# One in-place ring of five long slots for a grouped 1x1 convolution that streams 201 MB

## Chip, cores, metric

The kernel runs on one core of a Trainium2 chip. The metric is the device time of one execution in microseconds (us); the executions of one kernel quoted here differ by 0.03 to 0.7% (0.1% before, 0.3% after the change). "Span" is the length of the one execution that the profiler recorded; it is 1.7 to 2.2 us shorter than the time of the same execution.

## The reference

```python
# x: (1, 512, 512, 192) bf16, w: (1, 1, 4, 48, 48) bf16, out as x
xg = x.reshape(1, 512, 512, 4, 48)
out = einsum('bhwgc,gcd->bhwgd', xg, w[0, 0])     # four groups of 48 channels, per pixel
```

It is a per-pixel product with a block-diagonal 192x192 matrix. There are 262,144 pixels of 384 bytes: 100.66 MB have to come in and 100.66 MB have to go out.

## The kernel before

Pixels lie in SBUF 128 rows deep. A "column" is one pixel of each of the 128 rows (49 KB), and there are 2,048 columns. TensorE transposes eight columns at a time (a "pair" of two groups of four columns), VectorE copies the transposed data out of PSUM, TensorE multiplies, and ScalarE (ACT) casts the result into an output buffer. SyncE (SP) issues the loads, ACT the stores. Input and output each have a ring of 256 columns, in pieces of 64 columns, with small pieces at both ends.

```python
BIG = 64                       # columns of a piece: 64*384 B = 24,576 B per row, one packet
RCOLS = 256                    # columns of each of the two rings
HEAD = (4, 4, 8, 16, 32)
TAIL = (32, 16, 8, 4, 4)
# ... plan_pieces: HEAD, then 30 pieces of BIG, then TAIL, for loads and for stores
def rows_view(ap, p):          # a piece's pixels: row r gets p.size neighbouring pixels
    return ap[128*p.col:128*(p.col+p.size), :].rearrange("(p i) c -> p (i c)", p=128)
# ...
x_sb = sbuf("x_sb", [128, RCOLS*C]);  o_sb = sbuf("o_sb", [128, RCOLS*C])
# SP: a load waits until TensorE has transposed what lay in its place
for p in loads:
    wq.wait(t_done, (p.g1 - body + 1) // 2)
    sp.dma_start(ring_view(x_sb, p), rows_view(xf, p)).then_inc(ld_sem[p.key], 16)
# ACT: a cast waits until the store of what lay in its place has landed
for g in range(NG):
    wait_out_free(wq, g)
    wq.wait(mm_done, g + 1)
    while pending and pending[0][1] <= g:
        store(pending.pop(0)[0])
    act.copy(dst_in_o_sb, o_ps[...]).then_inc(fa_done, 1)
    if g in store_end:
        pending.append((store_end[g], g + ST_DELAY))
```

Of the kernel before, what the change touches and what calls it, by code (L numbers as in the profile page):

```python
# [6 lines left out]
BF16 = mybir.dt.bfloat16  # L7
# [4 lines left out]
C = GROUPS * CG  # L12
UC = 2 * C
# [8 lines left out]
ESHIFT = 112  # L22
ECOLS = 272

BIG = 64
RCOLS = 256
HEAD = (4, 4, 8, 16, 32)
TAIL = (32, 16, 8, 4, 4)
NXP = 4
NXS = 3  # L30
NOB = 4
ST_DELAY = 2


class Waiter:

    def __init__(self, eng):
        self.eng = eng
        self.seen = {}
# [7 lines left out]

class Piece:

    def __init__(self, col, size, key):  # L50
        self.col, self.size, self.key = col, size, key
        self.g0, self.g1 = col // 4, (col + size) // 4


def plan_pieces(cols, head, tail):
    sizes = list(head) if cols >= sum(head) + sum(tail) else []
    last = list(tail) if sizes else []
    mid = cols - sum(sizes) - sum(last)
    pieces, c = [], 0
    for s in sizes + [BIG] * (mid // BIG) + ([mid % BIG] if mid % BIG else []) + last:  # L60
        whole = s == BIG and c % BIG == 0
        pieces.append(Piece(c, s, ("big", c // BIG % (RCOLS // BIG)) if whole else ("own", len(pieces))))
        c += s
    return pieces


def bass_standalone__grouped__vision_kernel(nc, x, w, out):
    B, H, W_, Cx = x.shape
    assert Cx == C and tuple(w.shape) == (1, 1, GROUPS, CG, CG)
    npix = B * H * W_  # L70

    cols = npix // 128
    assert npix % 512 == 0, "the pixel count must be a multiple of 512"
    NG = cols // 4
    loads = plan_pieces(cols, HEAD, TAIL)
    stores = plan_pieces(cols, HEAD, TAIL)
    load_of = {p.g0: p for p in loads}
    store_at = {g: p for p in stores for g in range(p.g0, p.g1)}
    store_end = {p.g1 - 1: p for p in stores}

    xf = x.rearrange("b h w c -> (b h w) c")
    of = out.rearrange("b h w c -> (b h w) c")
    wv = w.rearrange("a b g c d -> c (a b g) d")

    body = RCOLS // 4
    NP = (NG + 1) // 2

    def groups(pair):
        return range(2 * pair, min(2 * pair + 2, NG))

    def rows_view(ap, p):
        return ap[128 * p.col:128 * (p.col + p.size), :].rearrange("(p i) c -> p (i c)", p=128)

    def ring_view(t, p):
        at = p.col % RCOLS
        assert at + p.size <= RCOLS
        return t[:, at * C:(at + p.size) * C]

    with ExitStack() as es:
        block = es.enter_context(nc.Block())  # L100
        x_sb = es.enter_context(nc.sbuf_tensor("x_sb", [128, RCOLS * C], BF16))
        o_sb = es.enter_context(nc.sbuf_tensor("o_sb", [128, RCOLS * C], BF16))
        xT_sb = [es.enter_context(nc.sbuf_tensor(f"xT_sb{i}", [128, 4 * UC], BF16)) for i in range(NXS)]
        ident = es.enter_context(nc.sbuf_tensor("ident", [128, 128], BF16))
        esel = es.enter_context(nc.sbuf_tensor("esel", [CG, ECOLS], BF16))
# [5 lines left out]
        def sem(name):  # L111
            return es.enter_context(nc.semaphore(name))

        ld_sem = {k: sem(f"ld_{k[0]}{k[1]}") for k in dict.fromkeys(p.key for p in loads)}
        st_sem = {k: sem(f"st_{k[0]}{k[1]}") for k in dict.fromkeys(p.key for p in stores)}
        ld_val, st_val, seen = {}, {}, {}
        for p in loads:
            seen[p.key] = seen.get(p.key, 0) + 16
            ld_val[p] = seen[p.key]
        seen = {}  # L120
        for p in stores:
            seen[p.key] = seen.get(p.key, 0) + 16
            st_val[p] = seen[p.key]
        w_sem, id_sem, e_sem, wb_sem, wc_sem = (sem(s) for s in ("w_sem", "id_sem", "e_sem", "wb_sem", "wc_sem"))
        p0_sem, p1_sem = sem("p0_sem"), sem("p1_sem")
        t_done, mm_done = sem("t_done"), sem("mm_done")
        e_done, fa_done = sem("e_done"), sem("fa_done")

        def wait_out_free(wq, g):
            if g >= body:  # L130
                p = store_at[g - body]
                wq.wait(st_sem[p.key], st_val[p])

        @block.gpsimd
        def _(gp):
# [11 lines left out]
        @block.sync  # L147
        def _(sp):
            wq = Waiter(sp)
            sp.dma_start(w_sb[:], wv).then_inc(w_sem, 16)  # L150
            for p in loads:
                wq.wait(t_done, (p.g1 - body + 1) // 2)
                sp.dma_start(ring_view(x_sb, p), rows_view(xf, p)).then_inc(ld_sem[p.key], 16)  # L153

        @block.tensor
        def _(pe):
            wq = Waiter(pe)

            def build_weights():
                wq.wait(e_sem, 1)  # L160
                wq.wait(w_sem, 16)
                last = None
                for (tc, r, g, c0_) in WBLOCKS:
                    s0 = ESHIFT - r
                    col = WOFF[tc] + c0_
                    last = pe.matmul(o_ps[:, NOB - 1, col:col + CG], lhsT=esel[:, s0:s0 + 128],  # L166
                                     rhs=w_sb[:, g, :], start=True, stop=True, skip_group_check=True)
                last.then_inc(wb_sem, 1)

            def transposes(pair):  # L170
                wq.wait(e_done, pair - 1)
                last = None
                for g in groups(pair):
                    p = load_of.get(g)
                    if p:
                        wq.wait(ld_sem[p.key], ld_val[p])
                    for ul in range(2):
                        u = g % body * 2 + ul
                        for tc in range(3):
                            col = u * UC + tc * 128  # L180
                            j = ul * 3 + tc
                            last = pe.transpose(xT_ps[:, g % NXP, j * 128:(j + 1) * 128],  # L182
                                                x_sb[:, col:col + 128], ident[:])
                last.then_inc(t_done, 1)

            def matmuls(pair):
                wq.wait(e_done, pair + 1)
                for g in groups(pair):
                    xs = xT_sb[pair % NXS][:, g % 2 * 2 * UC:(g % 2 + 1) * 2 * UC]
                    wq.wait(fa_done, g - 1)  # L190
                    last = None
                    for ul in range(2):
                        v = 2 * g + ul
                        for tc in range(3):
                            j = ul * 3 + tc
                            c0_, c1_ = COLR[tc]
                            last = pe.matmul(o_ps[:, v % NOB, c0_:c1_], lhsT=xs[:, j * 128:(j + 1) * 128],  # L197
                                             rhs=wt[:, WOFF[tc]:WOFF[tc] + (c1_ - c0_)],
                                             start=(tc == 0), stop=(tc == 2), skip_group_check=True)
                    last.then_inc(mm_done, 1)  # L200

            build_weights()
            wq.wait(id_sem, 1)
            transposes(0)
            wq.wait(wc_sem, 1)
            for pair in range(NP):
                if pair + 1 < NP:
                    transposes(pair + 1)
                matmuls(pair)

        @block.vector
        def _(dve):
            wq = Waiter(dve)
            wq.wait(wb_sem, 1)
            dve.tensor_copy(wt[:], o_ps[:, NOB - 1, 0:WCOLS]).then_inc(wc_sem, 1)  # L215
            for pair in range(NP):
                n = len(groups(pair))
# [6 lines left out]
        @block.scalar  # L224
        def _(act):
            wq = Waiter(act)
            pending = []

            def store(p):
                act.dma_start(rows_view(of, p), ring_view(o_sb, p)).then_inc(st_sem[p.key], 16)  # L230

            for g in range(NG):
                wait_out_free(wq, g)
                wq.wait(mm_done, g + 1)
                while pending and pending[0][1] <= g:
                    store(pending.pop(0)[0])
                v = 2 * g
                u = g % body * 2
                dst = o_sb[:, u * UC:(u + 2) * UC].rearrange("p (u c) -> p u c", u=2)
                act.copy(dst, o_ps[:, v % NOB:v % NOB + 2, 0:UC]).then_inc(fa_done, 1)  # L240
                if g in store_end:
                    pending.append((store_end[g], g + ST_DELAY))
            for (p, _) in pending:
                wq.wait(fa_done, p.g1)
                store(p)
            for p in stores:
                if st_val[p] == seen[p.key]:
                    wq.wait(st_sem[p.key], st_val[p])


# [26 lines left out]
```

## Time and profile before

| | before |
|---|---|
| time, median (range) | 489.41 us (489.05 to 489.53, 4 runs) |
| span of the profiled run | 488.1 us |
| TensorE / ACT / VectorE busy | 90% / 79% / 50% |
| bytes moved / mean rate | 202.2 MB / 414 GB/s |

First the parts of the page of the kernel before that say what the transfers did: the span cut into 40 slices (DMA busy in tenths, then GB/s), the queues, and the head of the chain of waits that ended last. Queue 1 carries the loads, queue 10 the stores, queue 8 instructions.

```profile
span 488.1 us, 13741 instructions
DMA  8999999999999999999999999999999999999793
GB/s 291 421 428 433 432 424 430 430 428 434 430 429 420 436 421 438 424 436 426 430 428 429 432 426 430 432 424 434 424 434 427 426 434 428 419 430 401 334 388 147
...
q10 hardware_dynamic: 5760, 100.67, 48.5%
q1 hardware_dynamic: 5968, 100.68, 48.5%
q8 instruction: 49, 0.80, 0.6%
q14 instruction: 10, 0.07, 0.0%
...
DMA 76%; PE 17%; ACT 3%; another core or an unknown queue 1%; issue 1%; SPq 1%; ACTq 0%
```

The rate is flat near 429 GB/s from the second slice on and falls only in the last four. 201.3 MB at 429 GB/s take 469 us, so 19 of the 488 us are start and tail. The chain of waits is 76% transfers.

Now the tail, in the view by stretches of 10 us of the kernel before. The columns are: length, busy us of TensorE matmuls (PE), weight loads, VectorE, ACT and GpSimd with counts, the granted clock, the mean busy share of the 16 DMA engines, GB/s.

```profile
210.00:220.00 10.00, 8.10 (x100) 7.48 (x99) 3.83 (x4) 7.16 (x10) 0.00 (x0) 0.83 1.00 429
220.00:230.00 10.00, 9.46 (x140) 8.41 (x138) 5.75 (x6) 8.56 (x12) 0.00 (x0) 1.00 1.00 427
...
450.00:460.00 10.00, 9.80 (x148) 8.92 (x146) 5.80 (x7) 9.09 (x13) 0.00 (x0) 1.00 0.92 386
460.00:470.00 10.00, 9.80 (x148) 8.92 (x147) 5.80 (x7) 9.13 (x13) 0.00 (x0) 1.00 0.76 318
470.00:480.00 10.00, 5.76 (x60) 4.70 (x57) 2.39 (x3) 4.55 (x6) 0.00 (x0) 0.75 0.62 260
480.00:490.00 10.00, 0.98 (x6) 0.64 (x6) 0.00 (x0) 1.61 (x3) 0.00 (x0) 0.50 0.39 153
```

In the bulk TensorE's busy time and even its clock may drop (210 to 220 us) and the DMA share stays at 1.00: the transfers do not wait for the compute. In the tail the mean share sinks, so some of the 16 DMA engines are already idle while others still work.

Who waited for whom in the kernel before (us in total, times, longest), and how long transfers took from issue to landing (median us in the last column):

```profile
ACT o_sb L240 <- DMA out_dram<-o_sb: 35.5, 21, 2.3
PE xT_ps L182 <- DMA x_sb<-in_x_dram: 6.5, 3, 3.9
SPq L153 <- PE xT_ps L182: 400.2, 31, 16.3
...
x_sb<-in_x_dram SPq DMA_DIRECT2D x30, 3072.0 KB, 27.1
out_dram<-o_sb ACTq DMA_DIRECT2D x30, 3072.0 KB, 45.2
```

A 3 MB store needs about 7.3 us at 429 GB/s, but lands after 45 us: several are queued. With a queue that deep the DMA engines were not short of work: their share is 1.00 to 1.03 in every 10 us from 50 to 430 us.

The trace keeps 16 completions of every transfer, and among the packets 16 of 4 bytes for each (656 of queue 1 for 41 loads, 640 of queue 10 for 40 stores). The last completion of all comes at 487.6 us, 0.4 us after the last packet. The completions of the third-last full-size store before the change are, relative to their median: first -6.2 us, second-last +2.2 us, last +9.6 us. One engine is alone at the end, from 484.2 to 487.2 us.

### The profile page before, as it was taken

The page shows a single profiled execution, that of the slowest core. Times are in us where ns is not written, and L with a number is a line of the kernel's source. Part 1 is how long each engine was busy: PE and PEld are TensorE (multiplying, and loading weights), DVE is VectorE, ACT ScalarE, POOL GpSimd, SP SyncE. Part 2 cuts the span into 40 slices and gives each one's busy share as a digit, 9 for nine tenths or more (in the row PEclk, how much of TensorE's full clock was granted, in tenths as well). Part 3 has the DMA queues.
Part 4 walks back from the last instruction along what each step waited for, and adds up shares of the span by engine and source line. Part 5 has one row for each costly group of instructions (what it writes and reads, how often), then busy time and mean ns, then how long its engine had stood idle before and what let it go on. Part 6 is the DMA issues. An engine that isn't in the chain of part 4 may idle for free.

```text
span 488.1 us, 13741 instructions
## 1 busy us (share of the span) xinstructions
PE 437.1 (90%) x6154; PEld 395.5 (81%) x6154; DVE 245.8 (50%) x257; ACT 387.4 (79%) x513; POOL 1.3 (0%) x8
## 2 busy tenths in 40 slices
PE   5999999988989899889899898899898989899963
PEld 5888888877978788778798787788787978789862
DVE  2555555555535455545455454545455535455530
ACT  2999998878878688868779687788687878699972
POOL 1000000000000000000000000000000000000000
PEclk9999999999989899989999899989899989899995
DMA  8999999999999999999999999999999999999793
GB/s 291 421 428 433 432 424 430 430 428 434 430 429 420 436 421 438 424 436 426 430 428 429 432 426 430 432 424 434 424 434 427 426 434 428 419 430 401 334 388 147
DMA packets 11787, 202.23 MB, mean 414 GB/s; under 512 B 1489, under 2 KB 2513, under 8 KB 3537
## 3 DMA queue, kind: packets, MB, share of 16 engines
q10 hardware_dynamic: 5760, 100.67, 48.5%
q1 hardware_dynamic: 5968, 100.68, 48.5%
q8 instruction: 49, 0.80, 0.6%
q14 instruction: 10, 0.07, 0.0%
HBM read 100.68 MB, written 100.66 MB: 412 GB/s over the span
## 4 chain that ended last, share of the span: by engine, by line
DMA 76%; PE 17%; ACT 3%; another core or an unknown queue 1%; issue 1%; SPq 1%; ACTq 0%
DMA out_dram<-o_sb 73%; PE o_ps L197 10%; PE xT_ps L182 7%; DMA x_sb<-in_x_dram 4%; ACT o_sb L240 3%; SPq L153 0%; ACTq L230 0%; SPq L150 0%; ACTq L45 0%
## 5 line engine op out<-in xcount | busy, mean ns | idle before, releaser
L240 ACT CAST o_sb<-o_ps 128x768 bf16<-128x768 f32 x512 | 386.1, 801 | 94.1 <-PE o_ps L197 51.2
L221 DVE COPY xT_sb<-xT_ps 128x1536 bf16<-128x1536 bf16 x256 | 245.2, 958 | 229.3 <-PE xT_ps L182 229.3
L197 PE MATMUL o_ps<-wt,xT_sb 128*128 128x144 bf16 (+1 forms) x3072 | 292.9, 239 | 34.8 <-ACT o_sb L240 30.3
L197 PEld LDWEIGHTS o_ps<-wt,xT_sb 128*128 128x128 bf16 x3072 | 213.6, 100 | 75.2 <-ACT o_sb L240 32.4
L182 PE MATMUL xT_ps<-ident,x_sb 128*128 128x128 bf16 x3072 | 222.1, 224 | 6.7 <-DMA x_sb<-in_x_dram 6.5
L182 PEld LDWEIGHTS xT_ps<-ident,x_sb 128*128 128x128 bf16 x3072 | 191.8, 100 | 7.6 <-DMA x_sb<-in_x_dram 4.4
L166 PE MATMUL o_ps<-w_sb,esel 48*128 48x48 bf16 x10 | 0.6, 210 | 2.6 <-DMA w_sb<-in_w_dram 2.6
L166 PEld LDWEIGHTS o_ps<-w_sb,esel 48*128 48x128 bf16 x10 | 0.4, 111 | 2.5 <-POOL esel L139 2.5
L215 DVE CAST wt<-o_ps 128x480 bf16<-128x480 f32 x1 | 0.7, 656 | 3.2 <-PE o_ps L166 3.2
L240 ACT ACT_TABLE_LOAD x1 | 1.3, 1283 | 0.8 <-PEq L262 0.8
L139 POOL TENSOR_SCALAR_AFFINE_SELECT esel<-esel 48x272 bf16<-48x272 bf16 x1 | 0.4, 406 | 0.0
L136 POOL MEMSET esel<- 48x272 bf16 x1 | 0.3, 318 | 0.3 <-POOLq L262 0.3
L143 POOL TENSOR_SCALAR_AFFINE_SELECT ident<-ident 128x128 bf16<-128x128 bf16 x1 | 0.3, 285 | 0.0
L137 POOL MEMSET ident<- 128x128 bf16 x1 | 0.2, 198 | 0.0
L262 POOL MEMSET const-bfloat16-1.0<- 128x1 bf16 x1 | 0.1, 102 | 0.0
L262 POOL MEMSET const-uint8-127<- 128x1 uint8 x1 | 0.1, 102 | 0.0
L262 POOL MEMSET const-float32-0.0<- 128x1 f32 x1 | 0.1, 98 | 0.3 <-issue 0.3
L262 POOL MEMSET const-float32-1.0<- 128x1 f32 x1 | 0.1, 98 | 0.0
## 6 DMA issues: line engine op xcount, KB each, us to landing
x_sb<-in_x_dram SPq DMA_DIRECT2D x30, 3072.0 KB, 27.1
out_dram<-o_sb ACTq DMA_DIRECT2D x30, 3072.0 KB, 45.2
x_sb<-in_x_dram SPq DMA_DIRECT2D x2, 1536.0 KB, 20.8
out_dram<-o_sb ACTq DMA_DIRECT2D x2, 1536.0 KB, 24.9
x_sb<-in_x_dram SPq DMA_DIRECT2D x2, 768.0 KB, 22.4
out_dram<-o_sb ACTq DMA_DIRECT2D x2, 768.0 KB, 19.6
x_sb<-in_x_dram SPq DMA_DIRECT2D x4, 192.0 KB, 27.2
x_sb<-in_x_dram SPq DMA_DIRECT2D x2, 384.0 KB, 25.1
```

The source lines that it names most:

```text
L136: gp.memset(esel[:], 1.0).then_inc(p0_sem, 1)
L137: gp.memset(ident[:], 1.0).then_inc(p1_sem, 1)
L139: gp.affine_select(out=esel[:], in_=esel[:], pattern=[[-1, ECOLS]], compare_op=AluOpType.is_equal, fill=0.0, base=ESHIFT, channel_multipli ...
L143: gp.affine_select(out=ident[:], in_=ident[:], pattern=[[-1, 128]], compare_op=AluOpType.is_equal, fill=0.0, base=0, channel_multiplier=1) ...
L166: last = pe.matmul(o_ps[:, NOB - 1, col:col + CG], lhsT=esel[:, s0:s0 + 128], rhs=w_sb[:, g, :], start=True, stop=True, skip_group_check=True)
L182: last = pe.transpose(xT_ps[:, g % NXP, j * 128:(j + 1) * 128], x_sb[:, col:col + 128], ident[:])
L197: last = pe.matmul(o_ps[:, v % NOB, c0_:c1_], lhsT=xs[:, j * 128:(j + 1) * 128], rhs=wt[:, WOFF[tc]:WOFF[tc] + (c1_ - c0_)], start=(tc == ...
L215: dve.tensor_copy(wt[:], o_ps[:, NOB - 1, 0:WCOLS]).then_inc(wc_sem, 1)
L221: dve.tensor_copy(xT_sb[pair % NXS][:, 0:n * 2 * UC].rearrange("p (g c) -> p g c", g=n), xT_ps[:, b0:b0 + n, 0:2 * UC]).then_inc(e_done, 1)
L240: act.copy(dst, o_ps[:, v % NOB:v % NOB + 2, 0:UC]).then_inc(fa_done, 1)
L262: nc = _bacc.Bacc("TRN2", target_bir_lowering=False, num_devices=1)
```

## The change

One ring of 520 columns takes the place of the two of 256: a result is cast over the input that it came from. Five slots of 104 columns make packets of 39,936 bytes instead of 24,576. The small pieces at the end go away: the last load is 72 columns, stored as 48 and 24. At the start four pieces take the place of five. A load now waits for the landing of the store that last used its slot.

```diff
-BIG = 64
-RCOLS = 256
-HEAD = (4, 4, 8, 16, 32)
-TAIL = (32, 16, 8, 4, 4)
+BIG = 104
+RCOLS = 5 * BIG
+HEAD = (8, 16, 32, 48)
+LAST = 24
@@ plan (cut) @@
+    stores = [(p, 0, p.size, p.g1) for p in pieces]
+    tail = pieces[-1]
+    if tail.full and tail.size > 2 * LAST:
+        cut = tail.size - LAST
+        stores[-1:] = [(tail, 0, cut, ...), (tail, cut, tail.size, tail.g1)]
@@ buffers @@
-        x_sb = ... [128, RCOLS * C];  o_sb = ... [128, RCOLS * C]
+        ring = ... [128, RCOLS * C]
@@ SP @@
-            for p in loads:
-                wq.wait(t_done, (p.g1 - body + 1) // 2)
-                sp.dma_start(ring_view(x_sb, p), rows_view(xf, p)).then_inc(...)
+            for p in pieces:
+                for q in pieces:
+                    if q.col < p.col + p.size - RCOLS and q.col + q.size > p.col - RCOLS:
+                        wq.wait(st_sem[q.i], st_val[q])
+                for dram, sbuf in transfers(xf, ring, p):
+                    sp.dma_start(sbuf, dram).then_inc(ld_sem[p.i], 16)
@@ ACT @@
             for g in range(NG):
-                wait_out_free(wq, g)
                 wq.wait(mm_done, g + 1)
-                (stores pending by ST_DELAY; casts into o_sb)
+                (casts into ring; a store goes out one group after its last cast)
@@ cut: option NARROW_AT for pieces on 32 rows only, empty here @@
```

## The prediction

> **What bounds the kernel now.** The DMA engines. The windows view at 10 us steps shows a DMA share of 0.97 to 1.04 and 426 to 435 GB/s in nearly every step from 50 to 430 us, whatever the compute does (PE busy swings between 8.0 and 9.9 us per step, ACT between 6 and 9). [...] x and out are 201.3 MB: 201.3 / 429 = 469 us of the 488 us span. The chain of waits says the same: 73% is store transfers, end to end, about 45 us each (three queued 3 MB pieces). ACT waits 35.5 us for output slots and SP 400 us for ring space; PE waits only 11 us for loads.
>
> The other 19 us: about 2 us before the first load packet, and the tail: from 440 us the DMA share falls 0.97, 0.92, 0.76, 0.62, 0.39. The landing records show why. The 16 engines drift apart: a late store's 16 completions spread over 16 to 18 us, and one engine is 7 to 9 us behind the second-last. On that engine packets follow each other without a gap to the end (487.2 us); so its own work, not the others' idle tail, sets the time. Likely extra work: instruction fetches (queue table: 49 packets of 16 KB, 0.6% of 16 engines, i.e. 47 us of engine time, unevenly spread).
>
> **What the change does.** Compute is unchanged: same matmuls, 256 DVE copies, 512 ACT casts, same instruction fetches. Bytes are unchanged.
> - Descriptors: packet records give 912 ns for 24,576 B, 121 ns for 3,072 B, 65 ns for 1,536 B: 27.2 B/ns plus about 8 ns each. A 39,936 B packet should take about 1.48 us (estimate). Per engine, 640 data packets become 376: 264 x 8 ns, about 2 us, plus 0.3 us of semaphore packets. That is all the steady state gains.
> - Tail loads of 32, 16, 8, 4, 4 columns go away. [...] So the last load will land about 448 us instead of 476, and the last cast end about 467 to 470 instead of 482. The 3.8 us wait near 472 us disappears. But this only fills the fifteen quicker engines; the slowest was already full. The end becomes a pure drain of stores.
> - The last store grows from 4 to 24 columns (1.2 MB, about 2.8 us), all bandwidth, not added latency.
> - In place, a load waits for a store's landing. Five slots are about 119 us of traffic at 23.8 us per slot; load about 41 us, compute 21.3 us (13 pairs x 1.64 us), store up to 54 us: about 116 to 119 us, so the load queue should not run dry. ACT's wait for output slots becomes small PE waits for loads (2 to 3 us per slot).
>
> **Sum.** 488.1 - 2.3 (descriptors) - about 0.5 (end) = about 485.5 us of span; the timed runs are 1.3 us above the span: 486.5 us, -0.6%.
>
> Chances: faster by over 2% 0.10, within 2% 0.87, slower 0.03.
>
> **Right if:** the DMA share stays at 1.0 through about 465 us; 39,936 B packets take 1.47 to 1.49 us; bulk GB/s rises under 1%; stores still chain; last completions still spread by several us.
>
> **Wrong if:** the laggard's extra time comes from small packets and not from instruction fetch (then up to 10 us more gain, about 477); long descriptors let fetches wait and starve PE; or the store-landing wait lets quick engines run dry and the laggard too (then 490 or more).

Two sentences are cut from it. Neither held a term of the sum, which stays 488.1 - 2.3 - about 0.5 = about 485.5 us of span and 486.5 us of time. The landing "about 448 us instead of 476" rests on the second of them: loads and stores take turns on an engine, packet by packet. The traces show it. In the kernel before, 4,375 packets of the two data queues from 100 to 400 us start as exactly one other packet ends (within 10 ns) and that one is of these queues; for 4,357 it is a packet of the other queue (in the changed kernel 3,108 of 3,113); and its last load of 192 KB, among store packets of 24,576 B, landed after 59.6 us. The about 0.5 us of the end and the 41 and 54 us of a load and a store are estimates; the medians measured after the change were 35.0 and 56.3 us.

## The result, and the profile after

| | before | after |
|---|---|---|
| time, median (range) | 489.41 us (489.05 to 489.53, 4 runs) | 487.07 us (486.67 to 487.94, 4 runs) |
| span of the profiled run | 488.1 us | 484.9 us |
| mean rate | 414 GB/s | 417 GB/s |

Ratios in this document are the mean time of one kernel's fast runs over that of the other's in the same rounds, so not quite the ratio of the medians. Here it is 0.9956, with a 95% interval of 0.9938 to 0.9973: 0.4% faster.

The same parts of the page of the changed kernel:

```profile
span 484.9 us, 13685 instructions
DMA  8999999999999999999999999999999999999982
GB/s 327 432 450 408 422 423 434 408 430 426 431 433 427 432 424 433 430 433 431 433 430 430 428 426 438 420 438 426 430 433 434 429 433 425 429 430 429 420 384 104
...
q1 hardware_dynamic: 3520, 100.68, 48.5%
q10 hardware_dynamic: 3456, 100.66, 48.5%
q8 instruction: 49, 0.80, 0.6%
q14 instruction: 8, 0.07, 0.0%
...
another core or an unknown queue 49%; DMA 23%; PE 21%; SPq 1%; ACT 0%; issue 0%
```

The packets of the two data queues fell by 4,752 (11,728 to 6,976), the instruction packets stayed at 49, and the bulk rate is still about 430 GB/s. Half of the chain is put down to an unknown queue: in order of time these are pieces of 23 to 25 us, each ended by the issue of the next load. Loads wait for landed stores here, so these are probably stores that the profile could not name; 10.2 MB of one slot at 429 GB/s are 23.8 us.

The tail by stretches, the waits and the landings of the changed kernel:

```profile
450.00:460.00 10.00, 9.90 (x149) 9.02 (x148) 5.95 (x7) 9.19 (x13) 0.00 (x0) 1.00 1.01 433
460.00:470.00 10.00, 3.09 (x40) 2.29 (x37) 1.32 (x2) 4.31 (x6) 0.00 (x0) 0.84 0.94 401
470.00:480.00 10.00, 0.00 (x0) 0.00 (x0) 0.00 (x0) 0.00 (x0) 0.00 (x0) 0.50 0.49 209
480.00:490.00 10.00, 0.00 (x0) 0.00 (x0) 0.00 (x0) 0.00 (x0) 0.00 (x0) 0.65 0.02 9
...
PE xT_ps L201 <- DMA ring<-in_x_dram: 29.1, 14, 3.1
SPq L173 <- DMA out_dram<-ring: 329.6, 14, 24.6
...
ring<-in_x_dram SPq DMA_DIRECT2D x18, 4992.0 KB, 35.0
out_dram<-ring ACTq DMA_DIRECT2D x18, 4992.0 KB, 56.3
```

The compute is over at 464 us (482 before), the DMA share stays full until then, and the last 20 us are stores alone. But the mean share of 0.49 and then 0.02 shows that most engines are done long before the last one: the third-last full-size store's completions lie at -6.4 us (first), +2.8 us (second-last) and +7.5 us (last). The straggler of before is still there. ACT's 35.5 us of waiting for output slots became 29 us of TensorE waiting for loads, about 2 us at each of 14 slots. With the DMA share at 1.0 through both, neither sets the time.

### The profile page after: what moved, and what is told of

Read it like the earlier page. It is cut to its first block, busy times and chain, and to the rows that moved or that the text cites. A ratio compares the mean times of both kernels' runs of the same rounds, so it can differ in the third digit from the quotient of the medians.

```text
span 484.9 us, 13685 instructions
## 1 busy us (share of the span) xinstructions
PE 427.3 (88%) x6154; PEld 388.6 (80%) x6154; DVE 245.7 (51%) x257; ACT 386.0 (80%) x513; POOL 1.3 (0%) x8
## 4 chain that ended last, share of the span: by engine, by line
another core or an unknown queue 49%; DMA 23%; PE 21%; SPq 1%; ACT 0%; issue 0%
DMA ring<-in_x_dram 13%; PE o_ps L216 12%; DMA out_dram<-ring 10%; PE xT_ps L201 9%; SPq L173 1%; ACT ring L259 0%; SPq L167 0%
## 5 line engine op out<-in xcount | busy, mean ns | idle before, releaser
L259 ACT CAST ring<-o_ps 128x768 bf16<-128x768 f32 x512 | 384.7, 802 | 77.7 <-PE o_ps L216 70.9
L216 PE MATMUL o_ps<-wt,xT_sb 128*128 128x144 bf16 (+1 forms) x3072 | 287.7, 237 | 4.5 <-ACT ring L259 0.4
L201 PE MATMUL xT_ps<-ident,ring 128*128 128x128 bf16 x3072 | 219.9, 223 | 29.1 <-DMA ring<-in_x_dram 29.1
L216 PEld LDWEIGHTS o_ps<-wt,xT_sb 128*128 128x128 bf16 x3072 | 210.0, 99 | 39.9 <-ACT ring L259 28.3
L201 PEld LDWEIGHTS xT_ps<-ident,ring 128*128 128x128 bf16 x3072 | 189.3, 100 | 32.2 <-DMA ring<-in_x_dram 28.1
## 6 DMA issues: line engine op xcount, KB each, us to landing
out_dram<-ring ACTq DMA_DIRECT2D x18, 4992.0 KB, 56.3
```

The lines of the kernel that those rows point to most:

```text
L201: last = pe.transpose(xT_ps[:, g % NXP, j * 128:(j + 1) * 128], xu[:, tc * 128:(tc + 1) * 128], ident[:])
L216: last = pe.matmul(o_ps[:, v % NOB, c0_:c1_], lhsT=xs[:, j * 128:(j + 1) * 128], rhs=wt[:, WOFF[tc]:WOFF[tc] + (c1_ - c0_)], start=(tc == ...
L259: act.copy(dst, o_ps[:, v % NOB:v % NOB + 2, 0:UC]).then_inc(fa_done, 1)
```

## Experiments

Theory A, the prediction's: the time is that of the slowest of the 16 DMA engines, which has work from start to end, and what makes it slow is the fetching of instructions through the same engines. (The runs bear out the first half. The second half does not hold for the engine that ends last, as the packet records show below.) Rivals: B, the memory's total rate is the limit and one engine is slow by nature; C, TensorE's reading of SBUF slows the transfers; D, the gain comes from the missing small pieces, not from the packets.

### The transfers alone

```diff
-   tensor, vector and scalar work per pair          (all of it)
-                wq.wait(fa_done, g1)                 # a store waits for its casts
+                wq.wait(ld_sem[p.i], 16 * len(p.blocks))   # ... for its load
```

> The changed kernel with all the per-pixel work of the engines taken out: each piece is loaded into the ring and stored back as soon as it has landed (wrong result on purpose, out = x). Same bytes, same pieces, same ring, hardly any instructions to fetch. Theory A (the time is that of the slowest of the 16 DMA engines, and what slows it is the fetching of instructions): instruction packets fall from 49 to under 10, the 16 completions of a late transfer lie within 3 us of each other instead of 13, the span falls from 484.9 to about 469 to 472 us (466 us of packets for one engine, 2 us of start, 2 us of last landing). Rival B (429 GB/s is what the memory gives all engines together, the compute side is irrelevant and one engine is slow by nature): the span stays at 478 to 485 us, one engine still ends 7 us or more behind.

The 466 us are an estimate, one engine's packets of the changed kernel at the median times of their sizes. The first load packet starts at 2.3 us there; the 2 us of last landing are the author's estimate (there the last completion comes 0.4 us after the last packet and the span ends 0.5 us later).

Measured: 472.16 us (ratio to before 0.9641, interval 0.9626 to 0.9655), span 470.6 us, wrong result. The lines of this kernel's page for the span and the queues (no instruction queue appears at all):

```profile
span 470.6 us, 118 instructions
GB/s 308 446 424 432 450 434 424 428 431 424 434 431 431 431 434 434 431 434 431 434 431 434 434 434 434 434 434 434 434 434 434 434 434 434 434 432 437 437 428 338
DMA packets 6976, 201.35 MB, mean 428 GB/s; under 512 B 960, under 2 KB 960, under 8 KB 1472
...
q1 hardware_dynamic: 3520, 100.68, 49.8%
q10 hardware_dynamic: 3456, 100.66, 49.5%
```

The third-last full-size store's completions lie within 2.3 us (-0.8, +1.3, +1.5). Without instructions no engine is slow by nature: that half of B falls. The other half, a limit on the memory's total rate, does not fit the end of the changed kernel: there the last engine works alone from 478.9 to 484.0 us, and its 9,216 B packets still take 347 ns each, the median of all engines' packets of that size. The same transfers with the compute take 14.3 us more span.

### The transfers plus a stream of matmuls that nobody waits for

```diff
+            for g in range(NG):                     # constants in, PSUM out, no semaphores
+                for j in range(6):
+                    pe.transpose(xT_ps[...], ident[:], ident[:])
+                for ul in range(2):
+                    for tc in range(3):
+                        pe.matmul(o_ps[...], lhsT=ident[:], rhs=wt[:, ...], ...)
```

> As the kernel with the transfers alone, plus a stream of 6144 matmuls of the same shapes that depends on nothing and that nothing depends on (they read constants; wrong result on purpose). Theory A: about 49 instruction packets are back, the late completions spread by 10 us or more again, the span is 481 to 486 us, though no transfer waits for any of this work. Rival B: no change from the transfers alone.

The same with 1,792 matmuls of 480 columns in place of the 6,144:

> As the transfers plus matmul stream, but the same streamed columns in 1792 matmuls of 480 columns instead of 6144 of 128 to 192: TensorE reads about as much and is busy about as long, with under a third of its instructions. Theory A (fetching): about 15 instruction packets, span 471 to 477 us. Rival C (what slows a DMA engine is TensorE's reading of the SBUF, not the fetching): 481 to 486 us as with the many small matmuls.

Measured: 484.61 us with the many matmuls (ratio 0.9898, interval 0.9882 to 0.9915), 475.00 us with the few wide ones (0.9701, 0.9686 to 0.9715), both with wrong results. The span and the queue of instructions, first of the kernel with many matmuls, then of the one with few:

```profile
span 482.7 us, 12407 instructions
PE 387.1 (80%) x6154; PEld 386.6 (80%) x6154; DVE 0.7 (0%) x1; POOL 1.3 (0%) x8
q8 instruction: 48, 0.79, 0.6%
```

```profile
span 473.3 us, 3703 instructions
PE 365.3 (77%) x1802; PEld 176.2 (37%) x1802; DVE 0.7 (0%) x1; POOL 1.3 (0%) x8
q8 instruction: 14, 0.23, 0.2%
```

TensorE's matmuls are busy about as long in both. Against the transfers alone the span is 12.1 us longer with the many (48 instruction packets) and 2.7 us longer with the few (14), and the late completions spread with them: third-last full-size store -8.4, +1.4, +5.1 us with many matmuls, -3.0, +1.7, +2.3 us with few. No transfer in these kernels waits for any matmul. By these two times alone C is not quite excluded, because the wide matmuls also load fewer weights (176 against 387 us).

The trace shows what an instruction packet costs. In the kernel with many matmuls, 47 of the 48 instruction packets start within 5 ns of the end of a load packet and 47 are followed, as they end, by a store packet that is longer than usual by about 399 ns. The instruction packets themselves take 1.02 us (median). So one packet takes about 1.4 us from one of the engines that carry the data. In the kernels before and after it is the same (46 and 47 of 49 are followed by a longer store packet).

But these packets are not what makes the last engine last. On one engine a packet's record starts 3 or 4 ns before the end of the packet ahead of it (about 15 ns behind an instruction packet), so the records can be sorted into sixteen chains, one for each engine. In the kernel with many matmuls they give three kinds of engine:

| engines | instruction packets on each | last packet ends, us | store packets |
|---|---|---|---|
| 7 | none | 468.4 to 468.7 | as usual |
| 8 | 6 | 476.6 to 477.2 | as usual, but for those behind instruction packets |
| 1 | none | 481.8 | longer by 102 ns (median) |

Without the compute all sixteen end between 468.4 and 469.8 us. So six fetched packets make an engine about 8.5 us late, and the engine that ends last, 13.3 us behind the seven, carries none. All its loss is in its data packets: its stores together are 11.4 us longer than usual, its loads 1.9 us. The kernels before and after have such an engine too, with none or at most one of the 49 instruction packets. What its packets lose from 45 to 430 us grows with the number of instructions that the kernel executes:

| kernel | instructions | loss of that engine, us | per instruction, ns |
|---|---|---|---|
| few wide matmuls | 3,703 | 4.0 | 1.1 |
| many matmuls | 12,407 | 13.3 | 1.1 |
| before the change | 13,741 | 13.9 | 1.0 |
| changed kernel, run again | 13,685 | 13.6 | 1.0 |
| with GpSimd's stream (below) | 19,317 | 21.8 | 1.1 |

Fetched packets grow with the same number, so the two times above could not tell the two apart. What lengthens this engine's packets the traces do not show. No run is known to be without the profiler's recording, so none shows these packets without it. C falls as a general slowing: seven engines end as early as without matmuls.

### Instructions that name no buffer

```diff
+            for pair in range(NP):                  # GpSimd, otherwise idle
+                gp.wait_ge(t_done, pair + 1)
+                for _ in range(10):
+                    gp.sem_inc(a_sem, 1)            # nobody waits for these two
+                    gp.sem_inc(b_sem, 1)
+                gp.sem_clear(a_sem)
+                gp.sem_clear(b_sem)
```

> The changed kernel, correct and unaltered in its transfers and its compute, with some 6,000 additional instructions on GpSimd, which is otherwise idle: per pair of groups 20 increments of two semaphores that nobody waits for, and their clearing. [...] 0.38 MB, 23 more instruction packets of 16 KB (72 instead of 49). Theory A, with the slope of the earlier runs (0.19 us per instruction packet from none to 14, 0.25 us from none to 48): 4 to 6 us slower than the changed kernel, span 489 to 491 us, ratio to the kernel before 1.002 to 1.006. Rival C (it is TensorE's reading of SBUF, its weight loads included, that slows the transfers): 485 us, ratio 0.994 to 0.9965. In between, if GpSimd's instructions are fetched by other DMA engines than the slowest.

The 0.38 MB are an estimate: the 0.80 MB of queue 8 for the 12,308 matmuls and weight loads of the changed kernel are 65 bytes each.

Measured: 500.49 us, correct (ratio 1.0230, interval 1.0216 to 1.0244), span 498.0 us: 13 us slower than the changed kernel, more than twice what I expected. The span, the DMA slices and the instruction queues of this kernel:

```profile
span 498.0 us, 19317 instructions
DMA  8999999999999999999999999999999999996950
q8 instruction: 49, 0.80, 0.6%
q14 instruction: 52, 0.43, 0.2%
```

GpSimd's instructions come through another queue (14), in 44 more packets of 8 KB, and in the third-last full-size store 14 engines are done by +1.2 us and two come at +21.4 and +24.8 us. Everything then hangs on these two, and the chains tell them apart. One carries the added packets: 36 of the 44 that queue 14 fetches from 45 to 430 us are on it (the other eight on two more engines, as in the changed kernel). Each takes 0.31 us and the load packet behind it is 0.35 us longer (medians), so 44 of them make it about 29 us late. Added to the 468.5 us of an engine that carries none (first table above), this gives 497.5 us; the last packet ends at 497.1 us. The other carries no instruction packet; it is the engine of the second table, with stores longer by 177 ns. So their fetching was not all that the added instructions cost, as I had assumed. The added instructions name no buffer in SBUF or PSUM (the diff above), and the transfers and the compute are the same. That fetching alone can make an engine late, and here the kernel with it, is therefore shown, in a kernel with a correct result. It depends on how the packets fall: 0.36 MB on one engine cost 29 us there, 0.79 MB of TensorE's on eight engines 8.5 us on each, which is less than the last engine loses in another way.

### Long packets against the rest of the change

Four kernels ran on one chip, five rounds each. First the in-place ring with pieces of 64 columns:

```diff
-BIG = 104;  RCOLS = 5 * BIG;  HEAD = (8, 16, 32, 48)
+BIG = 64;   RCOLS = 8 * BIG;  HEAD = (8, 16, 40)
```

> The changed kernel with pieces of 64 columns (24,576 B packets as before the change) in eight slots of one in-place ring; head 8, 16, 40; last store 24 columns as in the changed kernel. It keeps all of the change but the descriptor length. Theory A (packet cost of 8 to 8.5 ns each): 552 data packets per engine instead of 376, so 1.5 us slower than the changed kernel, ratio to the kernel before 0.998 to 1.000. Rival D (the gain is the missing small pieces and the ring, not the descriptors): as the changed kernel, 0.9956.

Measured: 488.68 us, correct, ratio 0.9972 (0.9958 to 0.9986). By the medians that is 1.45 us more than the in-place ring with four long slots on the same chip (487.23 us, below), as expected from 176 more packets per engine at 8.5 ns.

Then the two rings of before without the small pieces at the end:

```diff
-    loads = plan_pieces(cols, HEAD, TAIL)
-    stores = plan_pieces(cols, HEAD, TAIL)
+    loads = plan_pieces(cols, HEAD, ())
+    stores = plan_pieces(cols, HEAD, (40, 24))
```

> The kernel before with two rings, but without the small pieces at the end: loads end in a whole 64-column piece, stores in 40 and 24 columns. Bookkeeping of the engines' queues with packet times of the trace gives 1.2 us less than before: ratio 0.9970 to 0.9985. Rival D (small pieces are the whole gain): ratio 0.9956 as the whole change, 2.1 us.

Measured: 489.14 us, ratio 0.9985 (0.9972 to 0.9997), 0.6 us below the median of the kernel before, half of the 1.2 us that I expected. The result was wrong (relative error 0.25): each piece lays out pixels on rows by its own size, so a piece loaded as 64 columns may not be stored as two pieces of 40 and 24. The transfers have the sizes intended, so the time may stand, but only as a time. D as the whole explanation falls: most of the gain is not there.

Then the small pieces put back into the changed kernel:

```diff
-    ... [BIG] * (mid // BIG) + ([mid % BIG] if mid % BIG else [])
+    ... [BIG] * (mid // BIG) + [40, 16, 8, 4, 4]
```

> The changed kernel with the last 72 columns loaded and stored as 40, 16, 8, 4, 4. If only the packets count: 0.5 us slower, ratio 0.9965. With the queues' alternation by packet (small load packets each wait for a 1.48 us store packet, the last load lands near 476 us instead of 445, the compute and the last stores trail behind it): 3 to 4 us slower than the changed kernel, ratio 1.001 to 1.004, and the DMA share falls below 0.9 from about 460 us.

Measured: 490.38 us, correct, ratio 1.0012 (1.0000 to 1.0025): 3.15 us slower than the four-slot kernel on the same chip (487.23 us, below). The page's slices of this kernel:

```profile
DMA  8999999999999999999999999999999999999943
GB/s 340 426 435 415 438 424 434 420 431 443 415 433 429 437 420 428 440 425 430 430 440 422 427 434 427 433 425 440 423 433 428 431 430 427 428 426 430 427 205 138
```

The last two slices fall to 205 and 138 GB/s, against 384 and 104 with the single 72-column piece. This agrees with the two queues' turns, packet by packet, in the traces before and after the change (4,357 of 4,375 and 3,108 of 3,113 packets, beside the prediction): the tail's load of 768 KB, which 429 GB/s would move in 1.8 us, landed 14.5 us after the load ahead of it (454.7 after 440.2 us). It has eight packets on each engine, and eight times a 1.48 us store packet and its own 0.23 us are 13.7 us (an estimate from the packet medians of the kernels before and after). The last load landed at 480.8 us, where the changed kernel's single 72-column piece had landed at 445.3 us. With long packets a tail of small loads cost more here than with short ones (3.15 us, against the 0.6 us that leaving it out gained with packets of 24,576 B).

### How many slots

```diff
-RCOLS = 5 * BIG
+RCOLS = 4 * BIG      # and, in a run of its own, 3 * BIG
```

> The changed kernel with four slots of 104 columns. If the ring's fifth slot only lengthens the queues (load 35 us and store 56 us to land), it costs nothing: within 0.2% of the changed kernel (ratio 0.9945 to 0.9975), with stores landing in about 41 to 45 us and loads in about 28 us. If the load's wait for a landed store costs each slot something, it is slower by 1% or more.

> The changed kernel with three ring slots of 104 columns instead of five. A load (at half rate 23.8 us), the compute of a slot (21.3 us) and a store (23.8 us) with their landings and issues are about 73 us, more than three slots of 23.8 us = 71.4 us, and the compute has then no slack. I expect the load queue to run dry: 500 to 530 us, DMA share 0.90 to 0.96 in the steady state. If instead landing waits cost little, it stays within 2% of 485.

Measured: with four slots 487.23 us, ratio 0.9948 (0.9935 to 0.9960), indistinguishable from five. Its stores land after 35.7 us instead of 56.3 (I had expected 41 to 45), its loads after 33.3 us (28 expected). The fifth slot only lengthens the queue. With three slots: 549.29 us, ratio 1.1218 (1.1192 to 1.1245), correct; the waits and two stretches of that kernel:

```profile
PE xT_ps L201 <- DMA ring<-in_x_dram: 84.6, 17, 9.9
SPq L173 <- DMA out_dram<-ring: 437.4, 16, 28.6
...
420.00:440.00 20.00, 18.87 (x280) 16.97 (x278) 11.37 (x12) 17.25 (x24) 0.00 (x0) 1.00 0.83 330
440.00:460.00 20.00, 19.31 (x287) 17.34 (x284) 11.52 (x13) 18.41 (x26) 0.00 (x0) 1.00 1.01 393
```

Here the DMA share does fall in the middle of the kernel and TensorE waits up to 9.9 us for a slot. The direction was expected, the size (549 instead of 500 to 530 us) was not, and I have not accounted for the difference.

### Taking bytes from the slow engine

The kernel has an option to place pixels on 32 rows only. I assumed that four engines carry such a piece and the other twelve are relieved; nothing had shown it before these runs, and its ground is cut from the first expectation. ("Those four" there are these four engines; the 11 and 3.65 us are estimates from 27.2 B/ns.) The run with two narrow pieces then showed four engines late. I ran it with 16 of the 2,048 columns moved (one narrow piece), with 32 moved (two), and the changed kernel itself again, all on one chip:

```diff
-BIG = 104
+BIG = 100
-    (plan from HEAD, BIG and NARROW_AT)
+    sizes = 8, 16, 32, 44, eleven of 100, N, 36, seven of 100, 96     # N: 64 columns on 32 rows
+    sizes = 8, 16, 32, 44, six of 100, N, 36, six of 100, N, 36, six of 100, 44   # two of them
```

> The changed kernel once more, unaltered, as the measure for the two other runs of this call: ratio 0.994 to 0.9975 to the kernel before, span about 485 us.

> The changed kernel with slots of 100 columns and, in place of 16 of the columns of all 128 rows, one piece of 64 columns on 32 rows only (the same pixels in all, correct result). [...] Those four carry 11 us more, the other twelve 3.65 us less (16 columns in and out at 27.2 B/ns). Theory A (the slowest engine's own work is the time) and the four are among the quick ones, which end 12 to 13 us ahead: span 481 to 483 us, ratio 0.987 to 0.991, spread of the late completions under 8 us. If the slowest engine is one of the four: 494 to 497 us. If no single engine sets the time but the sum of the bytes: unchanged, 485.

> The same with two such narrow pieces: twelve engines carry 7.3 us less, four 22 us more. Theory A: the four are now the slowest and set the time: 468 + 22 us, span 488 to 493 us, ratio 1.000 to 1.010, with four engines late together. If narrow pieces simply help, another 3 us less than with one.

Measured: the changed kernel 486.80 us, ratio 0.9936 (0.9925 to 0.9948); with the first measure (0.9956) its gain is 0.4 to 0.6%. One narrow piece 486.29 us, ratio 0.9929 (0.9911 to 0.9946): no clear gain, where theory A promised 2 to 4 us. Its six runs differ more than those of the changed kernel, 485.22 to 487.88 us, and three of them lie at least 0.9 us below every run of the changed kernel (486.74 to 487.00 us). Two narrow pieces 502.74 us, ratio 1.0253 (1.0233 to 1.0272), slower than the 488 to 493 us expected, with four completions of the third-last full-size store at +12.0 to +15.5 us and the other twelve by +0.2 us. The last part bears out the first half of theory A: bytes put on four engines make exactly four late. That relief of the slow engine paid so little with one narrow piece has a visible part in its trace, which is that of the slowest of the six runs: in the next two loads four of the sixteen completions lag by about 17 us, TensorE waits once for 11.3 us, and the packets on all engines together are lengthened by 6.6 us per engine over the median of their size, against 3.7 us in the changed kernel run again. Why they lengthen stays open. No version beat the changed kernel clearly.

## Why the prediction was right

- **"The DMA engines" bind, and of these the slowest.** Shown. Without the compute the same transfers take a span of 470.6 us with all engines level; a matmul stream that nothing waits for brings back 12.1 us and the straggler; with added GpSimd instructions two engines are late by over 20 us, and the time follows them.
- **Descriptors, "about 2 us".** Shown. A 39,936 B packet was predicted at 1.48 us; the packets' median is 1.476 us. The medians of 65 ns for 1,536 B, 912 ns for 24,576 B and 1,476 ns for 39,936 B fit 27.2 B/ns plus about 8.5 ns a packet. Back at 24,576 B in the same kind of ring, with 176 of the 264 packets per engine put back, the time rises by 1.45 us.
- **Tail loads, "this only fills the fifteen quicker engines".** Shown for the kernel before: without its small pieces 0.6 us are gained. The last load landed at 445 us (predicted 448) and the last cast ended at 464 us (467 to 470). It does not hold in general: with long packets a tail of like small pieces costs 3.15 us.
- **The ring, "the load queue should not run dry".** Shown with room to spare: four slots do as well, three do not. The text reckoned that five slots were just filled (116 to 119 us); that was only the queues growing to the room they had.
- **The sum.** Span 485.5 us predicted, 484.9 us measured; time 486.5 predicted, 487.07 and 486.80 us measured. Descriptors (1.45 us) and tail (0.6 us) together make 2.05 us of the 2.3 us between the medians of the first measure (2.9 us in the second). The new pieces at the start were not tried on their own.
- **"Likely extra work: instruction fetches".** Wrong for the engine that ends last. The text took the instruction packets' own 47 us of engine time, "unevenly spread". They do cost what their engines carry, with 0.4 us more for the store packet behind each, but eight engines share them evenly and end about 8.5 us late, and the last engine carries none or at most one. Its own packets are longer, by about 1 ns for each instruction executed, and why stays open. The predicted number did not need this step: the loss is nearly the same before and after (13.9 and 13.6 us), so it drops out of the difference.

## What to carry to other kernels

When the mean DMA share is 1.0, look at the 16 completions of a late transfer before tuning anything: here the last of them, 7.5 us behind the median after the change, set the time, and the mean hid it. Longer packets are worth their saved overhead and no more, here 8.5 ns each. In a kernel that the DMA engines bind, instructions take transfer time too, even on an engine with time to spare: the same transfers took a span of 470.6 us alone, 473.3 us beside 3,703 instructions and 482.7 us beside 12,407. Fewer and wider instructions can so be worth more than better transfers (9.4 us of span between these two streams, 2.3 us of time from the whole change); no run here tried that in a kernel with a correct result. And where two possible causes grow together, as fetched packets and executed instructions do, sort the packets by engine before you name one.
